# Hashed attention and channel mix on one core: the second pair of heads joins the later pairs' way of making bits, under a new written-out order

## The chip, the cores and the metric

The kernel runs on one core of one Trainium2 chip. The metric is device time in microseconds of one launch; lower is better. Three runs of the kernel before gave 242.56, 242.76 and 243.35 us, median 242.76. A profile is one further execution, taken by the hardware profiler.

## What is computed

Two stages, one behind the other. The first is attention over 4 batches, 8 heads, 768 positions and 64 dimensions, in which a query sees only the keys of its own hash bucket. The bucket is the pattern of six sign bits of `q @ proj` and `k @ proj`:

```python
q_bits = einsum('bhsd,dk->bhsk', q, proj) > 0        # likewise k_bits
mask   = q_bucket[:, :, :, None] == k_bucket[:, :, None, :]
scores = where(mask, scale * q @ k^T, -1e9)
x      = softmax(scores) @ v                          # heads side by side: (4, 768, 512)
```

The second is a channel mix on that output, with `x_prev` being `x` shifted by one position:

```python
xk = mu_k * x + (1 - mu_k) * x_prev ; xr likewise with mu_r
out = sigmoid(xr @ w_r) * ((relu(xk @ w_k) ** 2) @ w_v)     # w_k 512x1024, w_v 1024x512, w_r 512x512
```

## The kernel before

**Pairs of heads.** Work is cut into 16 pairs of heads (`n` = 0 to 15, four to a batch). For a pair, the scores are made transposed, keys on the partitions, in nine steps of 1024 columns (`sc{n}_{s}`, L544): TensorE writes one of four PSUM slots of 1024 columns, and ScalarE takes the exponential into `pt` (`exp{n}_{s}`, L548). `add_pv` multiplies by the values (`oo`, L571), and VectorE divides (`rc`, `ob`). The result is transposed into `xt` (by TensorE for pairs 0 to 3 and 15, `ot`, L599; by a transposing DMA for the others), and `add_mix` forms `xk` and `xr`. When the four pairs of a batch are through, `add_moe` runs the channel mix: `kp` (L659), relu on ScalarE (L663), square on VectorE (L666), `r` (L679) and `v` (L692), then the output (L699) and its store.

**The mask as six more rows of the product.** The array `a` that TensorE multiplies holds, per position, 64 dimensions in float16 and in rows 64 to 69 the six signs as plus or minus a constant. Where all six agree, the product gains 6 x 4096, which the bias of the exponential takes away again; where one differs, the exponential is zero. A sign must come out as in float32, and there are two ways to make it.

*By float32 on TensorE* (`add_prep_turn`, L446, pairs 0 and 1, named in `FIRSTS`). VectorE casts to float16 (`hi`, L467). TensorE transposes the float32 input (`y`, L478), ScalarE evacuates it negated (`ey`, L483), TensorE multiplies it by the projection in float32 (`x`, L489), VectorE takes the sign bits (`ex`, L497) into `nh`, TensorE transposes `nh` in float16 (`t`, L512), and VectorE, or ScalarE for pair 0's keys, evacuates that to `a` (`evt`, L517 or L519). Pair 0 goes one head at a time, in four rounds; pair 1 both heads at once, in two (q and k).

*By a split in float16* (`add_prep`, L390, and `add_bits`, L414, pairs 2 to 15). VectorE writes the float16 value (`hi`, L398) and the remainder (`lo`, L401) side by side into `nh`; a transposing DMA turns it into `a` (`tr`, L405). TensorE multiplies `a` of both heads and both sides by the float16 projection and its remainder in one joined product (`bits`, L427, 16 matmuls into one of the four score slots), VectorE turns signs into constants (`bx`, L431), and GpSimd copies four times six rows into `a` (`row`, L443), one copy for each of q and k of head 0 and 1. Scores of a head wait for the rows of that head. Pairs 2 and 3 do hi, lo and tr for q and k apart; from pair 4 on they are joined.

**Start.** The first loads are pair 0's q and k in halves (L321) and the projection, followed in SP's queue by the later pairs' q and k (L330) and values (L335). TensorE meanwhile runs matmuls on a zeroed tile: 14 single ones (`warm0` to `warm13`, L246), which the transposes of `add_prep_turn` depend on, and eight steps of two (`warmb0` to `warmb7`, L251), which nothing depends on and which the order may put anywhere. In the order before, warmb0, 5, 4 and 3 stand among the single ones, warmb1 behind t0k0, and warmb6, 2 and 7 among the scores of pairs 2 and 3.

**Values.** For pairs 0 to 3 GpSimd casts the values (`va`, L350) and forms their sum in three steps (`vsum` a, b, c: L356, L359, L362); the product of the pair needs both.

**Order.** `Plan.add` numbers every step with its engine, what it reads and writes, and a cost. `Plan.schedule` then issues the steps in the written-out list `ORDER`, and `BANKS` gives each PSUM tile its place. Each engine executes its own steps strictly in that order; between engines only the dependencies hold. In the order before, TensorE's steps around pair 1 are: y1k0 behind x0k1; x1k0, y1q0, t1k1, t1k0, x1q0, t1q1, t1q0 among pair 0's scores; then the scores of pair 1, with bits2 behind the third of them.

Of the kernel before, what the change touches and what calls it, by code (L numbers as in the profile page):

```python
# [128 lines left out]
def kernel(  # L129
# [32 lines left out]
    PARTS = {0: ((0, 1), (1, 2)), 1: ((0, 2),)}  # L162
    W_CAST = ["POOL"] * 10
    MERGED = tuple(range(4, 16))
    FIRSTS = (0, 1)
    JOINT = ()
    OT_PE = (0, 1, 2, 3, 15)
    QS = 4.0
# [9 lines left out]
    def buf(shape, dt, name):  # L178
        return pool.tile(shape, dt, name=name, tag=name)
# [599 lines left out]
```

## Time and profile before

| | us |
|---|---|
| median of three runs | 242.76 |
| lowest, highest | 242.56, 243.35 |
| the profiled execution | 242.0 |
| its span, first to last instruction | 240.2 |
| granted TensorE clock | 1.000 |

Times within the profile count from the start of the span. A group of instructions is shown as line, engine, operation, output from input (buffer numbers left out), shape, then count, busy time, mean of one in ns, and the idle time ahead of them with what ended it. A row of the timeline gives start and length of a merged stretch of like instructions. A row of the chain that ended last gives start, length, engine and line. A row of a stretch gives its bounds and length, the busy time of TensorE's matmuls (PE), its weight loads (PEld), VectorE (DVE), ScalarE (ACT) and GpSimd (POOL) with instruction counts in brackets, the granted clock, and DMA share and rate.

### The profile page before, as it was taken

How to read it: one execution, taken by the hardware profiler on the slowest of the kernel's cores; microseconds unless marked ns; L12 is line 12 of the kernel's file. 1: busy time of each engine (PE TensorE's matmuls, PEld its weight loads, DVE VectorE, ACT ScalarE, POOL GpSimd, SP SyncE). 2: the span in 40 equal slices, each digit the busy share in tenths (PEclk: the TensorE clock that was granted, in tenths of full speed). 3: DMA queues.
4: the chain of work that ended last, by engine and by line, in shares of the span. 5: the costliest groups of instructions: out<-in, count | busy, mean ns of one | idle time of the engine just before them, and what ended most of it. 6: DMA issues, size and time to landing. Idle time of an engine off the chain costs nothing.

```text
span 240.2 us, 6251 instructions
## 1 busy us (share of the span) xinstructions
PE 234.1 (97%) x2515; PEld 147.8 (62%) x2532; DVE 179.8 (75%) x388; ACT 181.9 (76%) x242; POOL 99.7 (41%) x148
## 2 busy tenths in 40 slices
PE   8999999999999999999999999999999999999994
PEld 6985776776766565656456656665566564455442
DVE  3488789999998898989868896887167867348232
ACT  2699999999999999889779999677884640256320
POOL 4064979989934899438087302550000000000000
PEclk9999999999999999999999999999999999999999
DMA  6989999999999999988999989401500401210333
GB/s 225 304 222 274 232 242 260 279 197 362 279 253 284 273 213 294 249 302 206 276 163 241 249 177 234 136 0 26 173 0 3 120 3 44 87 46 1 131 135 131
DMA packets 72605, 44.00 MB, mean 183 GB/s; under 512 B 54912, under 2 KB 67584, under 8 KB 72576
## 3 DMA queue, kind: packets, MB, share of 16 engines
q1 hardware_dynamic: 72208, 43.20, 70.9%
q8 instruction: 20, 0.33, 0.6%
q10 hardware_dynamic: 368, 0.39, 0.5%
q14 instruction: 9, 0.07, 0.1%
HBM read 24.12 MB, written 6.29 MB: 127 GB/s over the span
## 4 chain that ended last, share of the span: by engine, by line
PE 92%; ACT 5%; issue 1%; DVE 0%
PE ps_all L544 25%; PE ps_all L692 17%; PE ps_all L659 16%; PE ps_all L571 14%; PE ps_all L679 8%; ACT pt L548 4%; PE ps_all L427 4%; PE ps_all L489 2%; PE ps_all L512 1%; PE ps_all L478 1%; ACT kr L663 1%; PE ps_all L251 1%; PE ps_all L246 1%; PE ps_all L599 1%; PE ps_all L566 1%
## 5 line engine op out<-in xcount | busy, mean ns | idle before, releaser
L548 ACT ACTIVATE pt<-ps_all 128x1024 bf16<-128x1024 f32 x144 | 138.4, 1041 | 10.9 <-PE ps_all L544 10.3
L544 PE MATMUL ps_all<-a 128*128 128x256 f16 (+1 forms) x384 | 79.2, 325 | 0.5 <-ACT pt L548 0.3
L443 POOL COPY a<-bx 6x384 f32<-6x384 f32 x56 | 38.9, 695 | 34.4 <-DVE bx L431 19.6
L544 PEld LDWEIGHTS <-a 128*128 128x128 f16 x384 | 34.0, 98 | 23.5 <-issue 4.6
L659 PE MATMUL ps_all<-xk,wk 128*128 128x384 bf16 x256 | 48.3, 326 | 0.1
L571 PEld LDWEIGHTS <-pt 128*128 128x128 bf16 x1152 | 42.5, 97 | 8.0 <-issue 0.5
L692 PE MATMUL ps_all<-wv,k 128*128 128x512 bf16 (+2 forms) x199 | 45.6, 362 | 0.5
L571 PE MATMUL ps_all<-va,pt 128*128 128x65 bf16 x1152 | 44.8, 193 | 0.0
L663 ACT ACTIVATE kr<-ps_all 128x384 bf16<-128x384 f32 x64 | 29.4, 491 | 16.0 <-PE ps_all L659 14.4
L659 PEld LDWEIGHTS <-wk 128*128 128x128 bf16 x256 | 24.2, 98 | 17.0 <-issue 0.6
L692 PEld LDWEIGHTS <-k 128*128 128x128 bf16 x208 | 19.3, 98 | 18.9 <-issue 0.3
L699 DVE SCALAR_TENSOR_TENSOR os<-rs,ps_all 128x512 f32<-128x512 f32 (+2 forms) x26 | 16.5, 643 | 19.0 <-PE ps_all L692 13.7
L682 ACT ACTIVATE rs<-ps_all 128x512 f32<-128x512 f32 x24 | 14.3, 602 | 20.5 <-PE ps_all L679 14.1
L666 DVE TENSOR_TENSOR k<-kr 128x384 bf16<-128x384 bf16 x64 | 23.2, 389 | 8.3 <-ACT kr L663 8.3
L401 DVE SCALAR_TENSOR_TENSOR nh<-nat,nh 128x1536 f16<-128x1536 f32 (+1 forms) x16 | 27.0, 1694 | 0.2
L679 PE MATMUL ps_all<-wr,xr 128*128 128x512 bf16 x88 | 23.2, 379 | 0.4
L356 POOL TENSOR_TENSOR vt<-vn 128x384 f32<-128x384 f32 x12 | 17.8, 1485 | 12.5 <-DMA vn<-in_v_dram 11.7
L589 DVE TENSOR_TENSOR ob<-ps_all,rc 128x384 bf16<-128x384 f32 x32 | 17.5, 553 | 1.4 <-DMA xt<-ob 0.8
L431 DVE TENSOR_SCALAR bx<-ps_all 128x768 uint16<-128x768 uint16 x14 | 13.4, 956 | 5.3 <-PE ps_all L427 4.7
L398 DVE TENSOR_SCALAR nh<-nat 128x1536 f16<-128x1536 f32 (+1 forms) x16 | 15.8, 985 | 0.3 <-PE ps_all L512 0.2
L679 PEld LDWEIGHTS <-xr 128*128 128x128 bf16 x96 | 9.0, 98 | 9.0
L380 DVE SCALAR_TENSOR_TENSOR va<-ps_all,vn 128x384 bf16<-128x384 f32 x24 | 12.7, 548 | 0.5 <-PE ps_all L375 0.2
(77 smaller groups left out, 188.9 us busy)
## 6 DMA issues: line engine op xcount, KB each, us to landing
vn<-in_v_dram SPq DMA_DIRECT2D x16, 384.0 KB, 5.1
out_dram<-os SPq DMA_DIRECT2D x23, 256.0 KB, 2.3
nat<-in_k_dram SPq DMA_DIRECT2D x15, 384.0 KB, 4.7
nat<-in_q_dram SPq DMA_DIRECT2D x15, 384.0 KB, 5.2
wst<-in_moe_w_k_dram SPq DMA_DIRECT2D x2, 512.0 KB, 7.0
wst<-in_moe_w_r_dram SPq DMA_DIRECT2D x2, 512.0 KB, 5.8
wst<-in_moe_w_v_dram SPq DMA_DIRECT2D x2, 512.0 KB, 4.4
k<-in_moe_w_k_dram SPq DMA_DIRECT2D x1, 512.0 KB, 4.4
```

The costliest lines, as they stand in the source:

```text
L356: e.tensor_tensor(out=vt[:, :, :, 0:E], in0=src[:, :, 0:3, 0:E], in1=src[:, :, 3:6, 0:E], op=ALU.add)
L401: nc.vector.scalar_tensor_tensor(out=nh[:, :, D:P], in0=nat.rearrange("p j (c d) -> p (j c) d", d=D), scalar=QS, in1=nh[:, :, 0:D], op0=AL ...
L443: nc.gpsimd.tensor_copy(side_a[side][n % NAQ][D : D + NB, j, :].bitcast(FP32), bx_t[sx][32 * i : 32 * i + NB, :].bitcast(FP32))
L544: nc.tensor.matmul(ps[:, lo - s * STEP : hi - s * STEP], side_a["k"][sa][:, j, jc * P : (jc + 1) * P], side_a["q"][sa][:, j, q0 : q0 + hi ...
L548: nc.scalar.activation(out=pt_t[sp][:, s * STEP : (s + 1) * STEP], in_=ps_t[plan.slot[nm]], func=AF.Exp, bias=EBIAS, scale=ESC)
L571: nc.tensor.matmul(oo[:, ic * 65 : ic * 65 + 65], pt_t[sp][:, o : o + P], va_t[sa][:, j, jc, 0 : D + 1], start=(not uc and ic == 0 and jc ...
L589: nc.vector.tensor_tensor(out=ob_t[so][:, :, j * D : (j + 1) * D], in0=oo[:, :, 0:D], in1=rc_t[sr][:, 1, :].unsqueeze(2).to_broadcast([P, ...
L659: nc.tensor.matmul(ps[:, 0:HALF], wk_sb[:, d, fc * P : (fc + 1) * P], xk_t[mx[d]][:, h * HALF : (h + 1) * HALF], start=(d == 0), stop=(d = ...
L663: nc.scalar.activation(out=kr_t[sk], in_=sm(nm)[:, 0:HALF], func=AF.Relu, scale=0.5 ** 0.5)
L666: nc.vector.tensor_tensor(out=k2_t[s2][:, h * HALF : (h + 1) * HALF], in0=kr_t[sk], in1=kr_t[sk], op=ALU.mult)
L679: nc.tensor.matmul(sm(nr), xr_t[mx[d]][:, c * P : (c + 1) * P], wr_sb[:, d, :], start=(d == 0), stop=(d == NDC - 1))
L692: nc.tensor.matmul(sm(nv)[:, x0:x1], k2_t[(b * NFC + fc) % NK2][:, c * P : (c + 1) * P], wv_sb[:, fc, x0:x1], start=(fc == 0), stop=(fc == ...
```

## The change

1. Pair 1 leaves `FIRSTS` and gets `hi`, `lo`, `bits`, `bx` and four `row` steps as pairs 2 and 3 have them. Its `nh` is not turned by DMA but by TensorE in float16 (four steps `t1q0` to `t1k1` of six transposes) with four evictions on VectorE. Its float32 transposes, evacuations, bit products and sign steps are gone.
2. `NWARM` goes from 14 to 8, and pair 0's transposes no longer depend on the warm-up. The eight steps of two matmuls stay.
3. The one-column exponential ahead of all others (`table`, L253), its tile `tb` and that tile's memset are gone; `nh` of one buffer instead of two is zeroed (`nz`).
4. `ORDER` (1332 steps before, 1323 after) and `BANKS` (350 before, 347 after) are new throughout.

```diff
-    NWARM = 14
+    NWARM = 8
...
-    FIRSTS = (0, 1)
+    FIRSTS = (0,)
+    TURNED = (1,)
...
-    tb = buf([P, 2], FP32, "tb")
     add("DVE", 0.2, lambda: nc.vector.memset(wz, 0.0), w=["wz"])
-    add("POOL", 0.1, lambda: nc.gpsimd.memset(tb, 0.0), w=["tb"], port=1, name="ctb")
...
-    add("ACT", 1.5, lambda: nc.scalar.activation(out=tb[:, 0:1], in_=tb[:, 1:2], func=AF.Exp), r=["tb"], w=["tb0"], at=0.75, name="table")
...
-    for i in range(NNH):
+    for i in range(1):
         add("DVE", 0.8, lambda i=i: nc.vector.memset(nh_t[i][:, :, D + NB : P].bitcast(FP32), 0.0), w=[("nz", i)], name=f"nz{i}")
...
             add("DVE", DVE_C(768 * m), lo, r=rn + nh_h, w=nh_l + [("nz", sh)], port=1, name=f"lo{n}")
+            if n in TURNED:
+                for j in range(2):
+                    nm = f"t{n}{side}{j}"
+
+                    def tp(nm=nm, nh=nh, j=j):
+                        ps = sm(nm)[:, 0:HALF].bitcast(FP16)
+                        for c in range(NSC):
+                            nc.tensor.transpose(ps[:, c * P : (c + 1) * P], nh[:, j * NSC + c, :], idh)
+
+                    def ev(nm=nm, a=a, j=j):
+                        nc.vector.tensor_copy(a[:, j, :], sm(nm)[:, 0:HALF].bitcast(FP16))
+                    add("PE", 0.48, tp, r=["idh", ("nhh", side, sh, j), ("nhl", side, sh, j)], w=[(nm,)], take=("sm", nm, 0), name=nm)
+                    add("DVE", DVE_C(S, 2), ev, r=[(nm,)], w=[("a", side, sa, j)] + [("ab", side, sa, j, h) for h in range(2)], give=[nm], name="ev" + nm)
+                continue
             add("SP", 1.86 if whole else 1.46, tr, r=nh_h + nh_l, w=ax, svc=2.95 if whole else 1.57, tr=1, name=f"tr{n}")
...
-                add("PE", 0.06 * 3 * m, tp, r=["idf", "warm", ("pt", 1, 8 * S // STEP)] + rn, w=[(ny,)], take=("sc" if whole else "sm", ny, 0), name=ny)
+                add("PE", 0.06 * 3 * m, tp, r=["idf", ("pt", 1, 8 * S // STEP)] + rn, w=[(ny,)], take=("sc" if whole else "sm", ny, 0), name=ny)
```

Read as names, the new order begins, engine by engine:

```
TensorE  warmb5 warm0 warmb2 warmb7 warmb1 warm1..warm6 y0q0 warm7 warmb6 y0k0 y0k1 y0q1 x0q0 x0k0
         warmb3 t0q0 t0k0 x0q1 x0k1 sc0_0 t0q1 sc0_1 t1q0 t1k0 t0k1 t1k1 sc0_2 sc0_7 warmb4 t1q1 sc0_3
         sc0_4 sc0_5 bits1 sc0_8 sc0_6 oo0_0 sc1_6 sc1_5 sc1_8 sc1_7 oo0_1 sc1_0 bits2 sc1_4 sc1_1 ot0
         sc1_3 sc2_3 sc1_2 sc2_2 ...                                       (warmb0 among pair 3's scores)
ScalarE  ey0q0 ey0k0 ey0q1 ey0k1 evt0k0 exp0_0 exp0_1 evt0k1 exp0_2 exp0_7 exp0_3 exp0_5 exp0_4 exp0_6
         exp0_8 exp1_6 exp1_8 exp1_5 exp1_7 exp1_0 ...
VectorE  hi0k0 nz0 hi0k1 hi0q0 hi0q1 ex0q0 hi1q ex0k0 lo1q evt0q0 ex0q1 hi1k ex0k1 lo1k hi2q evt1q0
         evt1k0 evt0q1 evt1k1 hi2k lo2q evt1q1 lo2k bx1 hi3q rc0 ob0 (head 0) hi3k mu_r lo3q lo3k
         rc0 ob0 (head 1) bx2 ...
GpSimd   constants, va0, three sums of pair 0, va1, first sum of pair 1, row1q1 row1k1 row1k0, second sum,
         row1q0, third sum, va2, two sums of pair 2, row2q0 row2k0 row2q1 row2k1 ...
SP       q0 (two halves), proj, q1, k1, mu_k, q2, v0, k2, v1, q3, mu_r, v2, k3, tr2q, tr2k, ...
         (before: q0, proj, k1, k2, mu_r, q2, k3, q1, v0, v1, q3, tr2q, tr2k, ...)
```

119 rows, old and new, of tables (BANKS, ORDER) are left out of this document.

## The prediction

> **What bounds the kernel now.** I read the page's busy shares first, then its chain that ended last.
>
> ```profile
> span 240.2 us, 6251 instructions
> PE 234.1 (97%) x2515; PEld 147.8 (62%) x2532; DVE 179.8 (75%) x388; ACT 181.9 (76%) x242; POOL 99.7 (41%) x148
> PE 92%; ACT 5%; issue 1%; DVE 0%
> ```
>
> Taken over the span, TensorE is the bound: 97% busy, and 92% of the chain. The change, however, lies in the first 25 us, so the next view is busy time by stretch: the start, pair 0's exponentials, attention alone, attention beside the first channel mix, the rest.
>
> ```profile
> 4.40:11.60 7.20, 7.20 (x76) 6.68 (x75) 3.35 (x11) 3.93 (x9) 0.89 (x4) 1.00 0.97 307
> 11.60:21.00 9.40, 9.40 (x88) 7.39 (x86) 7.70 (x15) 9.16 (x12) 6.19 (x9) 1.00 0.91 231
> 21.00:57.80 36.80, 36.77 (x588) 25.36 (x586) 33.93 (x60) 36.59 (x41) 30.44 (x36) 1.00 1.10 260
> 57.80:95.00 37.20, 36.71 (x462) 23.80 (x461) 34.49 (x69) 36.69 (x50) 27.94 (x31) 1.00 1.12 273
> 95.00:236.70 141.70, 140.83 (x1302) 82.25 (x1314) 98.68 (x234) 94.23 (x135) 31.76 (x48) 1.00 0.51 133
> ```
>
> After each stretch's length come PE, PEld, DVE, ACT and POOL. From 21.0 to 95 us ScalarE is as full as TensorE (36.59 of 36.80, 36.69 of 37.20); only after 95 us is TensorE alone. Which of the two sets the pace in the middle is seen in ScalarE's own timeline.
>
> ```profile
> 5.73 1.64 ACT L483 ACTIVATE pt<-ps_all 128x384 f32<-128x384 f32 x4 [2.19 <-PE ps_all L478]
> 7.23 0.22 ACT L253 ACTIVATE tb<-tb 128x1 f32<-128x1 f32 x1
> 8.31 0.80 ACT L519 COPY a<-ps_all 128x768 f16<-128x768 f16 x1 [0.85 <-PE ps_all L512]
> 10.19 0.81 ACT L483 ACTIVATE pt<-ps_all 128x768 f32<-128x768 f32 x1 [1.08 <-PE ps_all L478]
> 11.60 4.69 ACT L548 ACTIVATE pt<-ps_all 128x1024 bf16<-128x1024 f32 x5
> 16.13 0.85 ACT L483 ACTIVATE pt<-ps_all 128x768 f32<-128x768 f32 x1
> 16.82 2.00 ACT L548 ACTIVATE pt<-ps_all 128x1024 bf16<-128x1024 f32 x2
> 19.06 35.03 ACT L548 ACTIVATE pt<-ps_all 128x1024 bf16<-128x1024 f32 x38 [0.24 <-PE ps_all L544]
> L548 ACT ACTIVATE pt<-ps_all 128x1024 bf16<-128x1024 f32 x144 | 138.4, 1041 | 10.9 <-PE ps_all L544 10.3
> ```
>
> One exponential takes 1.041 us, but 38 of them fill 35.03 us without a gap: (35.03-1.04)/37 = 0.919 us from start to start. So from 19.06 to 54 us ScalarE never waits, and TensorE's stalls are hidden in its busy time. Channel-mix products can begin only when four pairs have passed ScalarE (57.8 us in the chain below, L659), and all TensorE work behind that point is queued up. The end therefore follows **the moment at which the stream of exponentials starts, and its gaps**. Pair 0 has nine exponentials; seven (x5 and x2) lie ahead of 19.06, so pair 1's first one starts at 19.06 + 2 x 0.919 = 20.9 us. That hand-over, 20.9 us, is the number that I carry forward.
>
> **What the change takes away.** On TensorE, pair 1's float32 transposes and bit products go. The chain that ended last has them one by one:
>
> ```profile
> 1.19 0.61 PE ps_all L251 x2
> 1.79 0.64 PE ps_all L246 x3
> 3.93 1.00 PE ps_all L246 x6
> 5.37 1.31 PE ps_all L478 x12
> 6.68 1.24 PE ps_all L489 x12
> 9.45 0.70 PE ps_all L478 x6
> 13.66 1.44 PE ps_all L489 x12
> 15.10 0.70 PE ps_all L478 x6
> 17.34 1.24 PE ps_all L489 x12
> 21.60 0.76 PE ps_all L427 x16
> 57.81 0.49 PE ps_all L659 x3
> ```
>
> (A float32 bit product counts twice: x12 is y's six or, for pair 0, two steps of three.) Removed: 0.70 + 0.70 + 1.24 + 1.24 (the 1.44 holds 0.2 of waiting) = 3.9 us. Added: one joined product, 0.76. Dummies that follow the first real step: four steps of two before, three now, 0.2 less. TensorE is spared 3.3 us. That would be the whole gain if TensorE set the pace there; by the part above it mostly doesn't.
>
> On ScalarE two evacuations of 0.81 and 0.85 go. The warm-up exponential of 0.22 us goes too; it ran while ScalarE waited 0.85 us for TensorE, and the table load stands under L483, ahead of it, so its removal is worth nothing. Were the load to move to the first exponential, it would cost its 1.28 us. The memset of nz1 (0.64 on VectorE, row below) and that of tb on GpSimd go from stretches where these engines have slack (3.35 of 7.20 and 0.89 of 7.20 busy): nothing.
>
> **The start, step by step.** Fifteen dummies precede the first transpose. At the half-rate spacing of the 0.64 row, 0.213 each, they end at 1.19 + 15 x 0.213 = 4.4 us. Before, the real work began at 5.37, behind the whole warm-up. The first key half had landed by 3.98, when VectorE took it:
>
> ```profile
> 3.98 0.36 DVE L467 TENSOR_SCALAR nh<-nat 128x384 f16<-128x384 f32 x1 [2.12 <-DMA nat<-in_k_dram]
> L401 DVE SCALAR_TENSOR_TENSOR nh<-nat,nh 128x768 f16<-128x768 f32 x4 | 3.7, 954 | 0.1
> L431 DVE TENSOR_SCALAR bx<-ps_all 128x768 uint16<-128x768 uint16 x14 | 13.4, 956 | 5.3 <-PE ps_all L427 4.7 <-ACT kr L663 0.7
> L517 DVE COPY a<-ps_all 128x768 f16<-128x768 f16 x6 | 3.3, 546 | 0.7 <-PE ps_all L512 0.4
> L497 DVE TENSOR_SCALAR nh<-ps_all 128x36 uint16<-128x36 uint16 x4 | 0.8, 191 | 3.2 <-PE ps_all L489 3.2
> L265 DVE MEMSET nh<- 128x696 f32 x2 | 1.3, 638 | 0.2
> 12.50 0.55 DVE L398 TENSOR_SCALAR nh<-nat 128x768 f16<-128x768 f32 x1
> 13.08 1.83 DVE L401 SCALAR_TENSOR_TENSOR nh<-nat,nh 128x768 f16<-128x768 f32 x2
> ```
>
> y0q0 ends near 4.9, three dummies at 5.3, the other three transpose steps (0.33 each, from 1.31 for four) at 6.3. x0q0 and x0k0 (0.62 each) end at 6.9 and 7.55. Behind ex0q0 the VectorE queue has hi1q (0.55), then ex0k0 (0.19): 7.8. t0q0 and t0k0 (0.35 each) end at 8.5, and evt0k0 on ScalarE (0.80) at 9.3. x0q1 and x0k1 stand ahead of sc0_0 in TensorE's order and end near 9.7; sc0_0 (0.43) lets the first exponential start at **10.2 us, 1.4 earlier than 11.60**. About 0.7 of it is that pair 1's ey1k0 no longer stands there, the rest the shorter warm-up.
>
> Pair 0's stream is then nine exponentials and evt0k1: 10.2 + 9 x 0.919 + 0.8 = 19.3 us. Pair 1 must be ready by then, or ScalarE waits.
>
> **What the change adds.** From ex0q0 at 7.0 us VectorE runs, in this order, what sc1_6 needs and what is queued ahead of it: four ex (0.19), four hi (0.55), four lo (0.95), six evictions (0.55), bx1 (0.96): 0.76 + 2.2 + 3.8 + 3.3 + 0.96 = 11.0 us, so bx1 ends at 18.0; start-to-start spacings a little below the busy means (0.91 for two lo in a row, row at 13.08) give 17.0 at best. Before, this stretch had 7.70 us of VectorE work in 9.40, so here the cover is used up. bits1 itself (0.76) hides behind lo2k; the PSUM slot that it takes among those of the scores is free by the spacing of the exponentials.
>
> Then come the row copies on GpSimd, and sc1_6 needs the first two:
>
> ```profile
> 23.58 4.82 POOL L443 COPY a<-bx 6x384 f32<-6x384 f32 x4 [2.77 <-issue]
> 49.89 2.40 POOL L443 COPY a<-bx 6x384 f32<-6x384 f32 x4 [0.57 <-POOL vt L356]
> 14.22 2.54 POOL L350 CAST va<-vn 128x768 bf16<-128x768 f32 x2 [7.66 <-DMA vn<-in_v_dram]
> 18.96 0.85 POOL L356 TENSOR_TENSOR vt<-va 128x390 f32<-128x390 bf16 x1
> ```
>
> Four take 2.40 to 4.82 us, so two take 1.2 to 2.4. With sc1_6 (0.43) the hand-over is ready between 17.0 + 1.2 + 0.45 = 18.7 and 18.0 + 2.4 + 0.45 = 20.9. It can't be before 19.3. Against 20.9 this is a gain between 1.6 and 0; I take 17.5 + 1.8 + 0.45 = 19.8, **1.1 us earlier**, since after bx1 VectorE soon waits for pair 0's output and the copies should be nearer the fast row.
>
> Later steps that move: pair 2's hi and lo end near 16 us, not 14.91, so its transposes go out about 1.5 us later; bits2 now stands behind sc1_0 at about 22.5 to 23.5, and rows 2 end for head 0 near 26 to 27. exp1_2, whose sc1_2 stands behind sc2_3, is due at 19.8 + 8 x 0.919 = 27.1: covered, narrowly; uncovered it costs up to 1.0. No DMA is added or removed; values move forward in SP's queue, past pair 3's keys.
>
> **The sum.** Hand-over -1.1, the rest of the stream as before, and the work behind 57.8 us the same (its new order could give or take about 0.5, the idle share of the last two stretches: 0.49 and 0.87). The profiled execution took 242.0 us, 1.8 more than its span; so 240.9 there. The median of the runs is 242.76, 0.76 above it: **241.6 us** (its own range 241.0 to 242.0).
>
> **A rule that speaks against it.** The dummies exist for the clock: spacing was 0.213 at 1.79 us, and the six of the row at 3.93 need 1.00, which is three at 0.213 and three at 0.11, so the full rate came at about 4.6, after 3.4 us of work. The Trainium skill, TensorE: Matmul & The Clock Gate, section Part 1: The HAM clock gate, says that full rate comes after one busy window of about 3.4 us, a window that runs freely; its Part 4 adds that transposes don't count as busy in the same way. The trace agrees with the first; no run here shows the second. As a mechanism of this kernel: with the dummies ending at 4.4, a transpose step stands in the window's last 0.2 us; if full rate came one such stretch later, half of 3.4 us, 1.7, would be lost ahead of the first exponential: 241.6 + 1.7 = 243.3. The page would have it so only if that 0.2 us decided. I give this 0.05.
>
> **Rivals.**
> TensorE sets the pace after all: then 3.3 us come off, 239.4. For it: its 97%, and the chain's 92%. Against: the gapless 38 exponentials. 0.13.
> The change does what it says, but off the path: VectorE's 11.0 us and slow copies put the hand-over back to 20.9 or so, 242.7. For it: pair 2's copies are of the slow kind (4.82). Against: VectorE's queue behind bx1. 0.20.
> Slower: GpSimd becomes late. va0, its three sums, va1 and vsum1a stand ahead of row1q1 in its order, and before, the same work ran from 14.22 (when values landed) to 18.96 + 0.85 = 19.8. The values are requested earlier now; if they still land no earlier, the two copies end between 21.0 and 22.2, the hand-over comes at 21.5 to 22.7, about 1.15 late at the middle: 243.9. It decides when GpSimd reaches row1q1 after 20.9 - 0.45 - 1.8 = 18.6 us; after 19.4 the loss is over 0.73. A milder form is hi1q waiting for its load ahead of ex0k0. 0.17.
>
> **Chances.** Forecast 0.45, TensorE 0.13, off the path 0.20, GpSimd 0.17, clock 0.05. A measurement of this kernel tells about 0.3% from no change, 0.73 us. Faster by over that: 0.45 + 0.13 = 0.58. Within: 0.20 + 0.05 = 0.25. Slower: 0.17. The range runs from 239.7 (most of the TensorE case is left out) to 243.7 (half of the GpSimd case is).
>
> **What would show it.** First exponential near 10.2 us; hand-over to pair 1 near 19.8 with a gap below 0.6 us ahead of it; bx1's end between 17.0 and 18.0; the first two row copies 1.2 to 2.4 us; va0 before 13 us; 3.3 us less float32 and dummy work on TensorE while the first channel-mix product moves by only about 1.1. If instead that product moves by 3, TensorE was the pace; if the copies start after 18.5, GpSimd's queue was mispriced; if the span moves and the hand-over doesn't, the order of the later work did it.

## The result, and the profile after

The changed kernel is slower: 244.01 us (median of 20 runs, 242.13 to 245.35) against 242.66 for the kernel before on the same chip (20 runs, 241.78 to 244.75), ratio 1.0043, 95% interval 1.0023 to 1.0064. Run again later it was 243.43 (12 runs), ratio 1.0026, interval 1.0001 to 1.0051. The forecast was 241.6 and faster.

Line numbers have moved: by 11 from `bits` on (L442 is `bx`, L454 the row copy, L559 the exponential), back by 3 ahead of it (L395 and L398 are `hi` and `lo`). In the experiments' kernels they stand 5 or 6 further on. The profiled execution took 244.44 us; its page begins:

```profile
span 242.5 us, 6217 instructions
PE 233.8 (96%) x2506; PEld 145.2 (60%) x2506; DVE 184.6 (76%) x388; ACT 181.1 (75%) x239; POOL 101.4 (42%) x151
```

TensorE is not longer busy than before, and yet the span has grown by 2.3 us: idle time has come in. The stretch from the hand-over region to the channel mix shows it (start, length, then PE, PEld, DVE, ACT, POOL):

```profile
11.60:21.00 9.40, 7.95 (x105) 5.31 (x104) 8.44 (x12) 8.42 (x10) 5.72 (x8) 1.00 0.78 214
21.00:57.80 36.80, 34.60 (x516) 23.21 (x513) 33.44 (x55) 35.81 (x40) 30.46 (x38) 1.00 1.12 251
```

TensorE has 1.45 and 2.2 us without work where it had none. ScalarE's timeline says where the stream of exponentials was cut (last brackets: idle time ahead of the stretch, and what ended it):

```profile
11.18 1.94 ACT L559 ACTIVATE pt<-ps_all 128x1024 bf16<-128x1024 f32 x2 [0.94 <-PE ps_all L555]
...
19.65 1.94 ACT L559 ACTIVATE pt<-ps_all 128x1024 bf16<-128x1024 f32 x2 [0.84 <-PE ps_all L555]
21.78 9.34 ACT L559 ACTIVATE pt<-ps_all 128x1024 bf16<-128x1024 f32 x10 [0.20 <-PE ps_all L555]
31.92 8.36 ACT L559 ACTIVATE pt<-ps_all 128x1024 bf16<-128x1024 f32 x9 [0.79 <-PE ps_all L555]
```

The first exponential starts at 11.18 (forecast 10.2, before 11.60). Two gaps of 0.84 and 0.20 stand ahead of the hand-over, which comes at 21.78, later than before. A gap of 0.79 follows ten exponentials on. A second execution of the same kernel, profiled later (its time 242.64), looks different up to the hand-over and the same behind it:

```profile
10.53 1.94 ACT L559 ACTIVATE pt<-ps_all 128x1024 bf16<-128x1024 f32 x2 [0.94 <-PE ps_all L555]
13.15 15.96 ACT L559 ACTIVATE pt<-ps_all 128x1024 bf16<-128x1024 f32 x17
29.91 11.11 ACT L559 ACTIVATE pt<-ps_all 128x1024 bf16<-128x1024 f32 x12 [0.79 <-PE ps_all L555]
```

Seven of the seventeen belong to pair 0; the eighth, pair 1's first, starts at 19.77. So the hand-over is **where the forecast had it, and still there is no gain**, since the gap of 0.79 stands there as well. A second profile of the kernel before (time 242.73):

```profile
11.78 4.69 ACT L548 ACTIVATE pt<-ps_all 128x1024 bf16<-128x1024 f32 x5
17.00 2.00 ACT L548 ACTIVATE pt<-ps_all 128x1024 bf16<-128x1024 f32 x2
19.45 21.19 ACT L548 ACTIVATE pt<-ps_all 128x1024 bf16<-128x1024 f32 x23 [0.45 <-PE ps_all L544]
```

Four milestones, read off the timelines exponential by exponential (the hand-over is the start of the 10th), show which part lost what:

| us | 1st exp. | hand-over | 20th exp. | 41st exp. | span |
|---|---|---|---|---|---|
| before, first profile | 11.60 | 20.89 | 30.01 | 49.37 | 240.2 |
| before, second | 11.78 | 21.27 | 30.40 | 49.75 | 240.9 |
| changed, first | 11.18 | 21.78 | 31.92 | 51.15 | 242.5 |
| changed, second | 10.53 | 19.77 | 29.91 | 49.14 | 240.6 |

From the 20th exponential to the end it is 210.2 and 210.5 before, 210.6 both times after: fixed by the order, some 0.3 longer in the new one. From hand-over to the 20th it is 9.12 twice before, 10.14 twice after: **+1.0, in both profiles**. From first exponential to hand-over it is 9.3 and 9.5 before, 9.24 or 10.60 after: **two patterns**. In the good one the hand-over gains 1.1 to 1.5 us, and 1.0 + 0.3 eat it; in the bad one it is 0.5 to 0.9 late as well. Of the 32 runs of the changed kernel 13 lie at or below 243.2 and 19 at 243.35 or above; the two profiled executions lie one on each side. No wide gap parts the two groups, so which pattern a run had is known for the profiled ones alone.

### The profile page after: what moved, and what is told of

Read it like the earlier page. It is cut to its first block, busy times and chain, and to the rows that moved or that the text cites. A ratio compares the mean times of both kernels' runs of the same rounds, so it can differ in the third digit from the quotient of the medians.

```text
span 242.5 us, 6217 instructions
## 1 busy us (share of the span) xinstructions
PE 233.8 (96%) x2506; PEld 145.2 (60%) x2506; DVE 184.6 (76%) x388; ACT 181.1 (75%) x239; POOL 101.4 (42%) x151
## 4 chain that ended last, share of the span: by engine, by line
PE 75%; ACT 9%; DVE 5%; POOL 4%; issue 4%; DMA 2%; SPq 1%; POOLq 0%; DVEq 0%; ACTq 0%
PE ps_all L555 18%; PE ps_all L670 17%; PE ps_all L703 16%; PE ps_all L582 11%; ACT pt L559 8%; PE ps_all L690 8%; PE ps_all L438 3%; DMA nat<-in_q_dram 2%; POOL a L454 2%; POOL wv L301 2%; DVE nh L398 1%; DVE nh L395 1%; DVE bx L442 1%; DVE a L419 1%; DVE a L528 0%
## 5 line engine op out<-in xcount | busy, mean ns | idle before, releaser
L559 ACT ACTIVATE pt<-ps_all 128x1024 bf16<-128x1024 f32 x144 | 138.9, 1041 | 14.3 <-PE ps_all L555 13.8
L555 PE MATMUL ps_all<-a 128*128 128x512 f16 (+1 forms) x384 | 80.2, 325 | 3.2 <-ACT pt L559 1.4
L454 POOL COPY a<-bx 6x384 f32<-6x384 f32 x60 | 42.8, 713 | 36.4 <-DVE bx L442 20.0
L703 PE MATMUL ps_all<-wv,k 128*128 128x512 bf16 (+2 forms) x208 | 46.4, 362 | 0.2 <-POOL wv L301 0.2
L677 DVE TENSOR_TENSOR k<-kr 128x384 bf16<-128x384 bf16 x64 | 23.8, 393 | 7.8 <-ACT kr L674 7.8
L398 DVE SCALAR_TENSOR_TENSOR nh<-nat,nh 128x1536 f16<-128x1536 f32 (+1 forms) x18 | 29.2, 1628 | 0.2
L690 PE MATMUL ps_all<-wr,xr 128*128 128x512 bf16 x96 | 24.0, 379 | 0.0
L353 POOL TENSOR_TENSOR vt<-vn 128x384 f32<-128x384 f32 x12 | 15.5, 1294 | 8.6 <-DMA vn<-in_v_dram 7.8
L395 DVE TENSOR_SCALAR nh<-nat 128x1536 f16<-128x1536 f32 (+1 forms) x18 | 16.4, 911 | 0.1
L442 DVE TENSOR_SCALAR bx<-ps_all 128x768 uint16<-128x768 uint16 x15 | 14.4, 958 | 2.8 <-PE ps_all L438 1.5
```

The costliest lines, as they stand in the source:

```text
L395: nc.vector.tensor_scalar(out=nh[:, :, 0:D], in0=nat.rearrange("p j (c d) -> p (j c) d", d=D), scalar1=QS, scalar2=None, op0=ALU.mult)
L398: nc.vector.scalar_tensor_tensor(out=nh[:, :, D:P], in0=nat.rearrange("p j (c d) -> p (j c) d", d=D), scalar=QS, in1=nh[:, :, 0:D], op0=AL ...
L454: nc.gpsimd.tensor_copy(side_a[side][n % NAQ][D : D + NB, j, :].bitcast(FP32), bx_t[sx][32 * i : 32 * i + NB, :].bitcast(FP32))
L555: nc.tensor.matmul(ps[:, lo - s * STEP : hi - s * STEP], side_a["k"][sa][:, j, jc * P : (jc + 1) * P], side_a["q"][sa][:, j, q0 : q0 + hi ...
L559: nc.scalar.activation(out=pt_t[sp][:, s * STEP : (s + 1) * STEP], in_=ps_t[plan.slot[nm]], func=AF.Exp, bias=EBIAS, scale=ESC)
L677: nc.vector.tensor_tensor(out=k2_t[s2][:, h * HALF : (h + 1) * HALF], in0=kr_t[sk], in1=kr_t[sk], op=ALU.mult)
```

## The experiments

Theory: three losses along one stream of exponentials, in (a) when TensorE reaches full rate, (b) VectorE's and GpSimd's work for pair 1 up to the hand-over, (c) pair 2's row copies. Rivals: a loss in TensorE's total, or in the later order alone. All edits move steps in the changed kernel's written-out order; nothing is removed from the computation.

### The start: dummies, and a load that VectorE waits for

```diff
 e1, TensorE
-warm6, y0q0, warm7, warmb6, y0k0
+warm6, warm7, warmb6, y0q0, y0k0
 e2, VectorE
-ex0q0, hi1q, ex0k0, lo1q, evt0q0, ex0q1
+ex0q0, ex0k0, evt0q0, hi1q, lo1q, ex0q1
 e3: both
```

> warm7 and warmb6 (three dummies) stand ahead of y0q0 instead of behind it; nothing else moves. In the changed kernel the four y steps ran from 4.36 to about 7.2 us, mostly at half rate. Theory clock (the transposes began before TensorE had reached full rate): the four y steps now end near 6.4, and if they are all that holds the start, the first exponential comes about 0.8 us earlier (10.4 instead of 11.18), the hand-over to pair 1 as well. Theory load (hi1q stands ahead of ex0k0 in VectorE's queue and waits until 8.15 us for its load): y ends earlier, but ex0k0 still comes at 8.6 and the first exponential stays within 0.2 us of 11.18; time unchanged within 0.3 us.

> hi1q and lo1q stand behind evt0q0 in VectorE's queue instead of ahead of ex0k0. Theory load: ex0k0 no longer waits for pair 1's load; it comes when x0k0 is done (8.4 us), so the first exponential is only about 0.2 to 0.3 us earlier as long as TensorE's half rate delays x0k0. Hand-over to pair 1 unchanged (21.8) if VectorE's whole queue up to bx1 sets it, since its sum is the same; 0.3 earlier if the first exponential does.

> Both edits: three dummies ahead of y0q0, hi1q and lo1q behind evt0q0. If each of the two waits covers the other, the first exponential comes near 10.2 to 10.4 us (0.8 to 1.0 earlier), more than the sum of the two alone. Theory VectorE queue (the work queued ahead of bits1 and bx1 sets the hand-over): the hand-over to pair 1 moves by less, 0 to 0.5 us from 21.78, and the time by as little. Theory start (the late first exponential is the whole loss): hand-over 0.8 to 1.0 earlier, time about 0.9 us below the changed kernel.

Measured: e1 243.37 (1.0035, 1.0008 to 1.0063), e2 244.91 (1.0079, 1.0050 to 1.0108), e3 244.8 (1.0085, 1.0057 to 1.0112). Profiles of e1, e2, e3: first exponential 10.64, 10.78, 11.18; hand-over 20.13, 20.89, 22.28; 20th 30.27, 31.02, 32.42. From hand-over to the 20th all three take 10.14, and to the span's end another 210.6: what happens in the start is carried to the end unchanged. Moving `hi1q` back only pushes pair 1's chain back. e1 is no worse than the changed kernel, and its interval overlaps; whether its dummies did anything can't be told, because the moment of full rate moves by itself. In the two executions of the unchanged order it shows in the float32 transposes, the first profile and the second:

```profile
4.36 0.85 PE L489 MATMUL ps_all<-pt,nat 128*128 128x128 f32 x3
5.64 1.59 PE L489 MATMUL ps_all<-pt,nat 128*128 128x128 f32 x9
```

```profile
4.36 0.62 PE L489 MATMUL ps_all<-pt,nat 128*128 128x128 f32 x3
5.14 1.15 PE L489 MATMUL ps_all<-pt,nat 128*128 128x128 f32 x9
```

The same twelve transposes took until 7.2 in one and 6.3 in the other: from start to start TensorE's matmuls are 0.21 apart up to about 6.5 us in the first profile and up to about 4.6 in the second, and 0.11 behind it. In both profiles of the kernel before, twelve fill 1.47 in one piece, since full rate came while the longer warm-up ran (4.5 and 4.9 us). With two profiles it is not shown that it always does.

### VectorE's order: pair 2's conversions, evt1q1

```diff
 e4, VectorE
-hi2q, ..., hi2k, lo2q, evt1q1, lo2k, bx1
+..., evt1q1, bx1, hi2q, lo2q, hi2k, lo2k
 e7, VectorE
-hi2k, lo2q, evt1q1, lo2k, bx1
+hi2k, evt1q1, lo2q, bx1, lo2k
 e8: e7, with e5 and e6 (below)
```

> Pair 2's hi and lo for q and k (4.8 us of VectorE in the changed kernel) and their transposing DMAs stand behind bx1 instead of ahead of it. Theory VectorE queue: bits1 no longer holds sc0_8 and sc0_6 back (evt1q1 near 13 to 14 instead of 17.2), bx1 ends near 16 to 17 instead of 19.65, the two waits of ScalarE of 0.84 and 0.2 us ahead of exponentials go, and the hand-over comes near 19.6 to 20.3 instead of 21.78; time 1.0 to 1.9 us below the changed kernel, unless pair 2's rows, now later, open a gap of their own of up to 1.5 us near 31 us. Theory start: hand-over stays within 0.4 us of 21.78.

> The changed kernel with VectorE's order changed: evt1q1, for which bits1 waits, ahead of lo2q, and lo2k behind bx1 (its transposing load behind it). Nothing is removed. Theory that the order on VectorE delays the hand-over: bits1 no longer waits 0.70 us, bx1 ends about 1.0 us earlier against the first exponential (from first exponential to hand-over 9.6 instead of 10.6 us), no gap of 0.84 ahead of the last two exponentials of pair 0; the time falls by 0.5 to 1.0 us if pair 2's lo2k, 0.9 us later, is still covered. Rival, that VectorE is full and whatever is put behind bx1 comes back as a gap of pair 2: hand-over earlier, but the gap ahead of the twentieth exponential grows from 0.79 to 1.5 or more, time unchanged.

> The three moves together: exp2_3 ahead of exp2_4, va1 and its first sum behind the row copies, evt1q1 ahead of lo2q and lo2k behind bx1. If the losses are separate terms of one stream, they add: first exponential to hand-over 9.3 us, hand-over to the twentieth exponential 9.3, time about 242.0 to 242.4, at or just below the kernel before. If VectorE's work is one budget, the sum is less than its parts: 242.8 to 243.5. If the later order alone made the loss, nothing changes: 244.

Measured: e4 245.97 (1.0138, 1.0097 to 1.018), e7 243.37 (1.0025, 1.0000 to 1.0050), e8 245.85 (1.0106, 1.0065 to 1.0147). e4's hand-over is at 20.04, against 21.78 in the first profile of the changed kernel, and the bill comes behind it:

```profile
20.04 3.77 ACT L564 ACTIVATE pt<-ps_all 128x1024 bf16<-128x1024 f32 x4 [0.61 <-PE ps_all L560]
24.47 1.02 ACT L564 ACTIVATE pt<-ps_all 128x1024 bf16<-128x1024 f32 x1 [0.66 <-PE ps_all L560]
26.00 1.02 ACT L564 ACTIVATE pt<-ps_all 128x1024 bf16<-128x1024 f32 x1 [0.51 <-PE ps_all L560]
```

Gap after gap: pair 2 is late by what pair 1 no longer waits for. e7 is the mild form. Its profile has the bad pattern, and the hand-over came 10.15 behind the first exponential (10.60 in the changed kernel); it came no earlier since three row copies, now beside `lo2k`, took 2.43 us instead of 1.80. e8's gaps (0.61 at the hand-over, 1.10 at pair 1, 0.74 at pair 2) are those of its parts.

### The order of pair 2's exponentials

```diff
 e5, ScalarE
-exp2_2, exp2_4, exp2_3, exp2_6
+exp2_2, exp2_3, exp2_4, exp2_6
 e10, ScalarE (sc2_0 ahead of sc2_1 too)
-exp2_2, exp2_4, exp2_3, exp2_6, exp2_5, exp2_1, exp2_0, exp2_7, exp2_8
+exp2_2, exp2_3, exp2_4, exp2_5, exp2_6, exp2_0, exp2_1, exp2_8, exp2_7
```

> The changed kernel with one instruction moved in ScalarE's order: exp2_3, whose scores need head 0 of pair 2 alone and are ready, goes ahead of exp2_4, which waits for all four row copies of pair 2. Theory that the wait is in the order (stream of exponentials sets the pace): the gap of 0.79 us ahead of exp2_4 is below 0.1, from the hand-over to pair 1 to the twentieth exponential it takes 9.2 to 9.4 us instead of 10.14, and the time falls by 0.8 us to about 243.2. Rival, that the gap is only passed on (the scores' slots or bits3 wait instead, or the rest of the order doesn't follow the stream): a gap of like size opens within the next ten exponentials, or the span stays 210.6 + 0.8 behind the twentieth exponential; time unchanged at 244.0.

> The changed kernel with the order of pair 2's exponentials and scores alone changed, now so that no two neighbours share a PSUM slot: exp2_3, 2_4, 2_5, 2_6, 2_0, 2_1, 2_8, 2_7 (in the earlier run exp2_6 came right behind exp2_4 and waited for its slot). Theory that the gap ahead of the twentieth exponential was a matter of this order: no gap above 0.3 us from the hand-over to the thirtieth exponential, and the span is 0.8 shorter than hand-over + 220.75, about hand-over + 219.95; time about 243.2. Rival, that the loss lies in TensorE's total or in the later order, whatever the stream does: the span stays at hand-over + 220.75, with the 0.8 us turning up as a gap later.

Measured: e5 243.56 (1.0032, 1.0006 to 1.0058), e10 243.46 (1.0034, 1.0008 to 1.0059). The rival held both times: in e5 a gap of 0.74 stands two places on, where sc2_6 waits for the slot of sc2_4. In e10, without that neighbour:

```profile
22.00 11.18 ACT L564 ACTIVATE pt<-ps_all 128x1024 bf16<-128x1024 f32 x12 [0.20 <-PE ps_all L560]
33.40 1.94 ACT L564 ACTIVATE pt<-ps_all 128x1024 bf16<-128x1024 f32 x2 [0.23 <-PE ps_all L560]
35.52 4.69 ACT L564 ACTIVATE pt<-ps_all 128x1024 bf16<-128x1024 f32 x5 [0.18 <-PE ps_all L560]
40.80 7.59 ACT L564 ACTIVATE pt<-ps_all 128x1024 bf16<-128x1024 f32 x8 [0.59 <-PE ps_all L560]
```

0.23 + 0.18 + 0.59 = 1.0 us comes back between the 22nd and the 29th exponential. So the gap is no accident of this order: the stream seems to catch up with something that comes at its own pace.

### Value work on GpSimd out of the way

```diff
 e6, GpSimd
-vsum0c, va1, vsum1a, row1q1, row1k1, row1k0, vsum1b, row1q0
+vsum0c, row1q1, row1k1, row1k0, va1, vsum1a, vsum1b, row1q0
 e9: va1 and its sums behind row1q0, va2 and its sums behind pair 2's rows
 e11: e9 and e10
```

> The changed kernel with two instructions of GpSimd moved: pair 1's value cast va1 and the first of its sums stand behind the row copies of head 1 and of k, q of head 0, ahead of the second sum. Theory that VectorE's chain is slowed by GpSimd working beside it: hi2k takes 0.55 us instead of 1.09 and lo2q about 1.0 instead of 1.6 (unless va0's sums now lie beside them), bx1 ends about 1.0 us earlier against the first exponential than in the changed kernel, and the time falls by 0.4 to 1.0 us. Rival, that VectorE's instructions are long for another reason (the loads landing beside them, or their own operands): their times stay at 1.1 and 1.6, bx1's end stays, and the time is unchanged or worse, as va1 now delays oo1 and the rows of pair 2.

> The changed kernel with GpSimd's order alone changed, this time with nothing ahead of a row copy: va1 and its sums behind all four row copies of pair 1, va2 and its sums behind all four of pair 2. Theory that VectorE's conversions are slowed by GpSimd's value work beside them: hi2k 0.55 and lo2q 0.95 to 1.2 us, bx1 ends 7.0 us or less behind the first exponential (8.5 in the changed kernel), first exponential to hand-over 9.1 to 9.3 us, no gap of 1.1 us at the fourth exponential of pair 1 (it came in the run before, where va1 stood ahead of the fourth row copy); the gap of 0.79 ahead of exp2_4 stays; time 243.0 to 243.4. Rival, that the value work is only moved beside other VectorE work (pair 0's output, pair 3's conversions, pair 2's row copies): bx2 or the row copies of pair 2 grow, and the gap ahead of exp2_4 grows by as much; time 244 or more.

> The two moves of this call together (value work behind the row copies, pair 2's exponentials reordered). If VectorE's slowed start and the gap ahead of the twentieth exponential are the two terms that lost the gain, first exponential to hand-over takes 9.1 to 9.3 us, there is no gap above 0.3 us up to the thirtieth exponential, and the time is 241.8 to 242.4, below the kernel before (242.6). If what is moved on GpSimd comes back in pair 2, 243.0 to 244.0.

Measured: e6 244.69 (1.0068, 1.0045 to 1.0092), e9 247.69 (1.0205, 1.0172 to 1.0237), e11 247.84 (1.0204, 1.0177 to 1.0231). In e6 `bx1` ended early (7.0 behind the first exponential), but the moved work stood ahead of `row1q0`, and a gap of 1.12 came at pair 1's fifth exponential (the next expectation calls it the fourth). Two things come out. First, what makes the bad pattern. VectorE's rows in the first profile of the changed kernel (`hi2q`, `hi2k`, `lo2q`, `bx1`), and then GpSimd's `va0`:

```profile
11.71 1.18 DVE L395 TENSOR_SCALAR nh<-nat 128x768 f16<-128x768 f32 x1
14.67 1.09 DVE L395 TENSOR_SCALAR nh<-nat 128x768 f16<-128x768 f32 x1
15.69 1.60 DVE L398 SCALAR_TENSOR_TENSOR nh<-nat,nh 128x768 f16<-128x768 f32 x1
18.68 0.96 DVE L442 TENSOR_SCALAR bx<-ps_all 128x768 uint16<-128x768 uint16 x1
```

```profile
11.59 0.88 POOL L347 CAST va<-vn 128x768 bf16<-128x768 f32 x1 [3.62 <-DMA vn<-in_v_dram]
```

The same steps in the second profile:

```profile
11.06 0.55 DVE L395 TENSOR_SCALAR nh<-nat 128x768 f16<-128x768 f32 x1
13.50 0.67 DVE L395 TENSOR_SCALAR nh<-nat 128x768 f16<-128x768 f32 x1
14.09 1.17 DVE L398 SCALAR_TENSOR_TENSOR nh<-nat,nh 128x768 f16<-128x768 f32 x1
16.68 0.94 DVE L442 TENSOR_SCALAR bx<-ps_all 128x768 uint16<-128x768 uint16 x1
```

```profile
11.51 0.82 POOL L347 CAST va<-vn 128x768 bf16<-128x768 f32 x1 [4.48 <-DMA vn<-in_v_dram]
```

`hi2q` takes 0.55 where it began ahead of `va0`, and 1.18 where it began 0.12 behind it. So in all profiles but e4's, where `hi2q` stands elsewhere: 1.11 to 1.18 in the six where `hi2q` (in e3, `hi1k`) began 0.11 to 0.41 us behind `va0`, 0.55 in the ten where it began first (0.73 in e17, where it began 0.51 behind). The rest follows in step: `hi2k` falls beside `va1`, `lo2q` beside its sum, and `bx1` starts 7.5 instead of 6.15 us behind the first exponential. e11 is the direct test, being in the bad pattern with `va1` and its sum moved away: `hi2q` 1.18, but `hi2k` 0.54 and `lo2q` 0.94, and the hand-over 9.53 behind the first exponential instead of 10.60. Second, in e9 the work that was moved is missed later:

```profile
39.29 1.02 ACT L564 ACTIVATE pt<-ps_all 128x1024 bf16<-128x1024 f32 x1 [1.72 <-PE ps_all L560]
43.01 5.75 ACT L564 ACTIVATE pt<-ps_all 128x1024 bf16<-128x1024 f32 x6 [2.70 <-PE ps_all L560]
```

Ahead of the first of these TensorE waits 3.13 us for pair 3's row copies (35.44 to 40.26), which stand behind all the values; then it works off its backlog. GpSimd has little room. Its busy time (last of the five) before and in the second profile of the changed kernel:

```profile
12.00:21.00 9.00, 9.00 (x82) 7.11 (x81) 7.48 (x14) 8.76 (x11) 6.19 (x9) 1.00 0.90 226
21.00:30.00 9.00, 8.98 (x138) 6.04 (x136) 7.37 (x11) 9.00 (x11) 6.18 (x6) 1.00 1.13 259
```

```profile
12.00:21.00 9.00, 8.72 (x103) 5.58 (x101) 7.83 (x15) 8.90 (x11) 8.04 (x12) 1.00 1.01 241
21.00:30.00 9.00, 7.68 (x117) 4.97 (x116) 7.25 (x10) 8.21 (x10) 8.54 (x9) 1.00 1.05 238
```

From 12.37 us of 18 it has gone to 16.58. Not all of this is work: at the shortest time that each of these instructions takes anywhere in these traces, they would need about 11.0 us, and 8.7 before. That is an estimate; the rest is stretching such as `va1`'s 1.55 us instead of 0.82.

### Pair 2's row copies

In the second profile of the changed kernel the chain that ended last runs through them. The first two copies take 0.50 each, from 24.99 to 26.04. Then the third and fourth, and VectorE's conversions for pair 4, `hi4` and `lo4` (1536 columns):

```profile
26.10 1.29 POOL L454 COPY a<-bx 6x384 f32<-6x384 f32 x1
27.44 1.92 POOL L454 COPY a<-bx 6x384 f32<-6x384 f32 x1
```

```profile
26.08 0.95 DVE L395 TENSOR_SCALAR nh<-nat 128x1536 f16<-128x1536 f32 x1
27.06 1.94 DVE L398 SCALAR_TENSOR_TENSOR nh<-nat,nh 128x1536 f16<-128x1536 f32 x1
```

Each of these copies began behind a conversion, by 0.02 and 0.38 us, and ended 0.36 us behind its end. (The view of the chain shows 1.26 us of the third copy as time in which GpSimd waits for nothing; the timeline shows that the copy was under way.) The scores that `exp2_4` needs follow on TensorE at 29.42, and the exponential starts at 29.91. In the kernel before pair 2's copies met `hi4` and `lo4` too (1.09, 1.12, 1.92 and 0.50 us), but there they were done at 28.39.

```diff
 e15, VectorE
-xs0, hi4, lo4, rc1, df0, xk0, bx3, ob1, rc1, ob1
+xs0, rc1, hi4, lo4, bx3, ob1, rc1, ob1, df0, xk0
 e13: bits2 in the slot of exp1_6, behind the first group of oo0_1; sc1_0 behind both;
      bx2 ahead of rc0, ob0 of head 1; row2 ahead of vsum2a, b
 e14: e13, va1 and vsum1a behind row1q0, vsum1b, c and va2 behind pair 2's rows
 e17: oo0_1 in the bank beside oo0_0; bits2 behind it in the slot of exp1_8, sc1_0 in that
      of exp1_5; row2 ahead of vsum2a, b
 e18: e17, va1 and its sums between pair 1's and pair 2's rows, va2 and its sums behind both
```

> The changed kernel with pair 2's chain moved forward: bits2 gets the slot that the first exponential of pair 1 frees (it had the third's) and stands behind the first group of oo0_1, bx2 ahead of pair 0's second division, the four row copies ahead of pair 2's and the rest of pair 1's value sums. Theory that bits2's slot and GpSimd's queue made pair 2 late: rows 2 land 6 to 7.5 us behind the hand-over (9.7 in the changed kernel), the gap of 0.79 ahead of the twentieth exponential is below 0.1, the time falls by 0.8 us against the changed kernel, to 242.6 to 243.2, and the best runs lie below the best of before (241.8). Rival, that GpSimd's total is the limit in this stretch: the gap vanishes there and opens at pair 3 (ahead of exp3_3 or next to it) with 0.5 us or more; time unchanged, 243.4 to 244.0.

> As e13, and va1 with its first sum behind pair 1's four row copies, its other sums and va2 behind pair 2's four. If the start is slowed by value work beside VectorE: first exponential to hand-over 9.1 to 9.3 us even when the first exponential is late, time 0.3 to 0.8 below e13. If GpSimd's total is the limit: gaps at pair 2 or pair 3 as in the two earlier runs that moved value work (1.7 and 2.7 us there), time over 244.5.

> The changed kernel with VectorE's order alone changed: pair 4's wide conversions hi4 and lo4 behind the first division of pair 1 (and pair 4's transposing load behind them), the token-shift differences df0 and xk0 behind bx3 and the divisions. Theory that pair 2's row copies stand still beside these conversions (in the second profile two copies take 0.50 each, then 1.26 us pass in which GpSimd waits for nothing shown, then two take 1.93): the four end 2.4 to 2.8 us after their start instead of 4.4, the gap of 0.79 is gone, time 0.8 below the changed kernel, 242.6 to 243.2, unless pair 4 is now late. Rival, that the copies are slow whatever VectorE does: 4.4 us again, gap unchanged, time 243.4 to 244.5.

> The changed kernel with pair 2's chain moved forward in another way: oo0_1 in the bank beside oo0_0, where nothing waits for a slot of the scores; bits2 behind it in the slot of pair 1's second exponential, sc1_0 in that of the third; row copies of pair 2 ahead of its value sums. If pair 2's lateness was the rest of the loss: no gap above 0.2 us from hand-over to the fortieth exponential, hand-over to twentieth exponential 9.2 to 9.3 us (10.2 in the changed kernel), span = first exponential + 9.2 + 9.3 + 210.6 where the values land behind hi2q, 239.2 to 239.8, and 1.4 more where they land beside it; time 242.2 to 243.0, best runs near 241.0. If the loss is in GpSimd's and VectorE's total, a gap of 0.5 or more opens elsewhere and the time is 243.3 to 244.

> As e17, with va1 and all of its sums between pair 1's and pair 2's row copies, va2 and its sums behind pair 2's. If the start's second pattern (VectorE's conversions beside value work, 1.4 us) comes from va1 and its sum: first exponential to hand-over 9.1 to 9.4 us in the profile, the median falls by 0.3 to 0.6 against e17. If GpSimd's queue is full there, row copies of pair 2 or 3 are late and it is slower than e17 by 0.5 or more.

Measured: e13 243.45 (1.0022, 0.9995 to 1.0049; best run 241.81), e14 245.12 (1.0086, 1.0055 to 1.0118), e15 243.88 (1.0050, 1.0021 to 1.0079), e17 243.15 (1.0031, 0.9999 to 1.0062), e18 248.9 (1.0250, 1.0219 to 1.0281). In e15 the four copies no longer meet wide conversions, and from hand-over (19.30) to the 20th exponential it is 9.23: mechanism (c) is shown as the cause of the gap there. First GpSimd, then ScalarE of e15:

```profile
24.51 2.18 POOL L459 COPY a<-bx 6x384 f32<-6x384 f32 x4
```

```profile
19.30 20.53 ACT L564 ACTIVATE pt<-ps_all 128x1024 bf16<-128x1024 f32 x22 [0.17 <-PE ps_all L560]
40.03 1.02 ACT L564 ACTIVATE pt<-ps_all 128x1024 bf16<-128x1024 f32 x1 [0.20 <-PE ps_all L560]
41.45 1.02 ACT L564 ACTIVATE pt<-ps_all 128x1024 bf16<-128x1024 f32 x1 [0.39 <-PE ps_all L560]
42.83 17.94 ACT L564 ACTIVATE pt<-ps_all 128x1024 bf16<-128x1024 f32 x19 [0.36 <-PE ps_all L560]
```

2.18 us instead of 4.38, no gap of 0.79, and 0.95 us lost in pair 3's exponentials instead: bits4, in TensorE's order ahead of those scores, now waits 0.48 us for pair 4's transposing load, and two transposes behind it wait 0.48 and 0.40 for VectorE. e13 also has its copies in 2.18 and no gap there, but one of 0.67 at exp1_0, which I had put behind bits2. e14, with value work moved behind the rows, has gaps of 2.01 and 1.21 at pair 2 beside that. e17 avoids the gap at exp1_0, and has none from hand-over to the 28th exponential, and then

```profile
22.16 17.72 ACT L565 ACTIVATE pt<-ps_all 128x1024 bf16<-128x1024 f32 x19 [0.18 <-PE ps_all L561]
40.76 22.81 ACT L565 ACTIVATE pt<-ps_all 128x1024 bf16<-128x1024 f32 x24 [0.89 <-PE ps_all L561]
```

Pair 3's copies were late, since pair 2's sum, now beside `hi4` and `lo4`, took 2.24 us instead of 0.85, and then the copies fell beside the next pair's conversions (36.14 to 40.99). The profiled execution of e17 took 245.61, the median being 243.15; TensorE's clock was at half in it from 10.74 to 14.15, so that its start is not typical. e18's moved values made pair 3 later still (gaps of 2.79 and 2.66).

### Both kernels once more

> The changed kernel itself once more, for a second profile. If the part behind the twentieth exponential is fixed by the order and all variation lies ahead of it, the span is 210.6 us (within 0.15) behind the start of that exponential, wherever this lies (31.9 in the first profile), and the full rate of TensorE comes at another moment than 6.4 us, the first exponential moving with it; time 243.5 to 244.3. If the later part varies as well, the distance differs by over 0.3 us.

> The kernel before once more, for a second profile. If its variation, too, lies ahead of the twentieth exponential, the span is 210.1 us (within 0.2) behind that exponential's start, and this start lies anywhere from 29.9 to 32; its hand-over follows its first exponential by 9.3 us whatever the start. If it is steadier than the changed kernel, first exponential and full rate lie within 0.3 us of the first profile's (11.60, 4.6).

Their profiles stand in the result. The changed kernel kept 210.6 from the 20th exponential to the end, as in the first profile, with that exponential 2.0 us earlier. The kernel before kept 210.2 and 210.5, and its 20th exponential moved by 0.4 only.

No version beat the kernel before; e17 (243.15) and e13 can't be told from it.

## Why the prediction was wrong

**What bounds the kernel: right.** In every one of the kernels the span follows the 41st exponential by 190.8 to 191.7 us, whatever the start did. The work that TensorE was spared turned up as idle time, and the first channel-mix product came at 60.67 and 58.67 us, no earlier than before (57.64 and 58.29).

**First exponential at 10.2 (-1.4): right in the shorter warm-up, 0.3 to 1.0 too hopeful, since a load was left out.** It came at 10.53 and 11.18. The chain that ended last runs, in the second profile and in the first, through pair 1's load of q, for which `hi1q` waits ahead of `ex0k0`:

```profile
2.27 5.23 DMA nat<-in_q_dram
```

```profile
2.26 5.89 DMA nat<-in_q_dram
```

`hi1q` starts at 7.52 and 8.17, and the first exponential follows by 3.01 in both. In the second profile x0k0 ended at 7.53, as foretold (7.55); the load alone made `ex0k0` 0.4 late. In the first, full rate at 6.5 instead of 4.6 held x0k0 until 8.47, which would have made it nearly as late without the load. So the milder form of the GpSimd rival held, and the clock rule that I gave 0.05 was real: I had read one execution as the rule. (e2 showed that moving `hi1q` costs more.) The eighteen profiles of the changed order and its variants have the first exponential from 9.99 to 11.61 and, by the granted clock recorded in their traces, full rate from 3.87 to 7.02 us. That the moment runs freely, as the Trainium skill says (TensorE: Matmul & The Clock Gate, Part 1: The HAM clock gate), is borne out; the scatter of 0.5 us either way that the page gives is too small for these profiles.

**VectorE's chain, bx1 at 17.0 to 18.0, hand-over 19.8: right in one pattern, wrong in the other.** Second profile: `bx1` ends at 17.62, hand-over 19.77. The near hit is partly luck: the copies were done at 19.01, earlier than forecast, and the stream, 0.3 late from its start, set the 19.77. First profile: 19.64 and 21.78. The failing term is 11.0 us from ex0q0 to the end of `bx1`, made of undisturbed durations (0.55, 0.95): it took 10.7 in the second profile and 11.8 in the first. My own rows had shown the disturbed ones (four row copies in 2.40 or in 4.82; in the same profile a `hi` of 1.17 at 16.94), and I took them for scatter. The foretold copies (1.2 to 2.4 for two) took 1.24.

**"Pair 2's rows: covered, narrowly; uncovered it costs up to 1.0", and "the rest of the stream as before": this is the step that failed.** I had checked the rows of head 0 alone, for exp1_2. That check held: in the second profile they were done at 26.04 (forecast 26 to 27), and exp1_2 started at 27.18 (forecast 27.1) without a gap. Two exponentials on, exp2_4 needs the rows of head 1 as well, and these two copies I had not timed. Beside `hi4` and `lo4` they took 1.29 and 1.92 instead of 0.50, and the last landed 9.6 us behind the hand-over (7.5 before), at 29.36 against 28.39 and 28.77: the stream came 1.1 to 1.5 us earlier, its supply did not. The cost was 1.02 from the hand-over to the 20th exponential. Closing that gap (e5, e10, e13, e15, e17) opened another each time, and the 41st exponential never came earlier than 49.1 us in any kernel, against 49.37 and 49.75 before. What paces the stream there is, I think, VectorE and GpSimd together, serving pairs 2 to 4; that is argued from the gaps that moved and from GpSimd's 16.58 of 18 us, not shown by taking work off these engines, which wasn't tried.

**GpSimd's rival: right engine, wrong place.** Values landed 2.5 to 2.7 us earlier than before (`va0` at 11.5, foretold "before 13"), so they didn't hold up pair 1's copies; they got beside VectorE's conversions instead.

**The later order: +0.1 to +0.5**, within the 0.5 that the prediction left open, on the wrong side.

The sum: +0.3 for the order, +1.0 at pair 2, and a hand-over 1.3 early in 13 of 32 runs and 0.7 late in 19 (if the runs divide at 243.3 as the two profiles do), -0.1 on average: +1.2. The medians differ by 1.35 in the first comparison and 0.49 in the second, the means by 0.94 and 0.61, so the sum has the sign and comes out rather too large. (The forecast's own sum gives 241.66, written as 241.6.)

The rows of the trace and a rule of the Trainium skill agree here, SBUF — State Buffer, section "Who interferes with whom": VectorE and GpSimd share one pair of ports, and where a VectorE instruction needs it, whichever started first holds it for its whole instruction and the other is blocked. Rows: 0.55 or 1.18 by who came first, `va1` 0.82 or 1.55 with the roles turned, copies that end 0.36 us behind the conversion beside them, while VectorE's evictions from PSUM keep 0.55 in both patterns. It would have told me which of the added operations could not be priced alone.

## What to carry to other kernels

Where VectorE and GpSimd both read and write SBUF in one stretch, price their sum, and look in the trace for two lengths of the same instruction: the longer one may be a collision, which here a shift of half a microsecond brought. When a change brings a consumer forward, compute the absolute time of the next two pairs' supplies as well, to the last of them and not the first; if these don't move, the gain ends there. One profile is one draw of the start: before resting a forecast of 0.5% on a moment in the first 10 us, ask whether that moment is set by the program at all.

## What the runs showed of the hardware

A long gap in TensorE's work had a price beyond its length: in e9 TensorE had work for only 1.41 of the 4 us from 36 on, and the granted clock, third from the end, was then 0.89 and 0.68 before it came back:

```profile
36.00:40.00 4.00, 1.41 (x16) 1.05 (x17) 3.31 (x3) 2.28 (x3) 3.83 (x4) 0.89 1.11 355
40.00:44.00 4.00, 4.00 (x71) 3.48 (x69) 0.00 (x0) 1.30 (x3) 2.53 (x6) 0.68 1.11 185
```

The clock record has one piece of 3.41 us at half rate there, from 39.12 on. Such pieces begin during or just behind TensorE's waits of 1.91 us (e14), 2.5 (e4; e11, twice as long there), 3.13 (e9) and 4.15 (e18), none at those of 1.71 (e6) and less; the changed kernel's own waits are at most 0.74, and it stayed at 1.00. Where between 1.71 and 1.91 the limit lies, or whether the share of time with work decides, wasn't tested. One case doesn't fit: e17's piece at 10.74, ahead of which TensorE had work for all of 3.4 us. Its cause is open.
